# A folded two-layer network after linear attention: high parts before low parts in the second product, output copies at other places, last weight sums earlier

## The chip, the cores and the metric

The kernel runs on one core of one Trainium2 chip. The metric is the device time of one launch in microseconds (us). Before the change three runs gave 1134.80, 1135.37 and 1135.81 us, median 1135.37 us. TensorE is called PE here, its weight loads PEld, VectorE DVE, ScalarE ACT, GpSimd POOL, and the engine that issues the transfers SP.

## The reference

```python
def phi(x):
    proj = np.einsum('bhsd,df->bhsf', x, w_phi)
    proj = proj - np.max(np.abs(proj), axis=-1, keepdims=True)
    return np.concatenate([np.exp(proj), np.exp(-proj)], axis=-1)
q_p, k_p = (phi(q), phi(k))
kv = np.einsum('bhsf,bhsd->bhfd', k_p, v)
z = np.sum(k_p, axis=2)
num = np.einsum('bhsf,bhfd->bhsd', q_p, kv)
den = np.einsum('bhsf,bhf->bhs', q_p, z)[..., None] + 1e-06
x = num / den            # 4608 tokens x 512 after a transpose
h = x @ w_in             # 512 -> 2048
out = (h - np.tanh(h)) @ w_out   # 2048 -> 512
```

There are 8 batches of 8 heads with 576 positions and 64 channels; the weights of the two layers arrive in double precision and are turned into f32 on the chip.

## The kernel before, in words

A first stage does the attention and decodes the weights; its last matmul ends at about 329 us. All that the change touches lies behind it, in the two layers, which are one loop over 72 steps `s`. The 4608 tokens are 9 groups `g` of 512 (four token tiles `t` of 128), and the 2048 hidden columns are 16 tiles `f` of 128. A step is one group and one pair `j` of hidden tiles, so a group is 8 steps. Instructions stand on each engine's queue in the order in which this code writes them (the schedule is manual), and each engine takes its queue in order.

**The first product** of a step is h = x W_in. Every operand is split into a high part, rounded to the fast matmul type, and a low part, the rest; a product is high times high, high times low and low times high. Groups 0 and 1 (steps 0 to 15, "plain") do it straight: `plain`, 12 matmuls of 512 columns for each hidden tile. Groups 2 to 8 (steps 16 to 71, "folded") cut it into 2 x 2 blocks and form it from seven products instead of eight: `product`, 42 matmuls of 256 columns a step, with sums of input blocks (made on POOL, `x_sum`) and sums of weight blocks (made once on DVE, `t_add`, and split by ACT in `t_hi` and by DVE in `t_lo`). DVE puts the seven results together in PSUM (lines 884 to 893). The sums of weights for the pairs j = 0 to 7 are made in steps 9, 10, 11, 12, 13, 14, 15 and 19 by the job table at line 817.

**The activation** h - tanh(h) is worked out for two sets a step: `one` (in PSUM tile `y` or `w`) and `two` (in `x` or `v`). In a folded step set one is token tiles 0 and 1 for both hidden tiles and set two is token tiles 2 and 3; in a plain step set one is the first hidden tile for all four token tiles and set two the second. For each set ACT makes squares (`y_`, `s1_`, `s2_`), tanh (`th_`) and a mask (`mk_`), and DVE joins a polynomial with h - tanh(h) (`d1` to `d5`, lines 610 to 622). ACT then rounds the result to its high part `gh` (line 626), and POOL subtracts for the low part `gl` (line 630). The order on DVE in a step is: d3, d4, d5 of the set two of the step before; the queued weight work (`v0`: `t_lo`; `d1`: `t_add`); in a folded step the joining of the seven products; d1 to d5 of the new set one; d1, d2 of the new set two. So set two is finished in the step after.

**The second product** adds g W_out into four PSUM tiles `po`, one a token tile, over the 8 steps of a group. It is done one step late, by the function `q`: for each token tile of a set the matmuls of `gh` with the high and low weights (line 654), then those of `gl` with the high weights (line 657). 24 matmuls of 512 columns a step. In a folded step `q(one, 1)` puts tile 0 between the third-to-last and the last of the seven products:

```python
for n in (3, 2):
    product(r[n], g, j, n)
if s < NS - 1:
    q(one, 1)
product(X[:, lo_], g, j, 4)
```

and the rest follows behind the product. With the last pair of a group the four `po` are complete; `finish` copies them out at the end of that step's code, tiles 0 and 2 on DVE (line 668), 1 and 3 on ACT (line 666), and each copy is followed by its transfer to `out`. The next group's first `q` writes the same four PSUM buffers, a step later. W_out comes anew from HBM for each step of group 1 and later (`wo_fetch`, two tiles of 512 KB, four buffers).

## Time and profile before

| what | value |
|---|---|
| median of three runs | 1135.37 us (1134.80 to 1135.81) |
| time of the profiled execution | 1136.19 us |
| span of its instructions | 1134.4 us |
| PE busy | 1113.2 us, 98% |
| DVE busy | 964.5 us, 85% |
| ACT busy | 860.4 us, 76% |
| POOL busy | 525.5 us, 46% |
| granted PE clock, mean | 0.998 |

Matmuls overlap in PE's pipeline and their ends are modelled, so a busy PE is not PE at its peak, and starts are a better measure than busy time. In the views a row of the timeline is start, duration, engine, line, operation, output and inputs, with the idle time before it and what ended it in brackets; a row with x4 joins four instructions. The view of waits is who waited for whom: us in total, times, longest.

### The profile page before, as it was taken

To read this page: it belongs to the slowest core of one execution; us is meant where nothing else is said; L and a number is where in the kernel's file an instruction comes from. 1 tells how busy PE (TensorE), PEld (TensorE's weight loads), DVE (VectorE), ACT (ScalarE), POOL (GpSimd) and SP (SyncE) were. 2 spreads that over 40 slices of the span, in tenths; PEclk is the share of its full clock that TensorE was granted. 3 is DMA by queue.
4 is the path that set the end of the run, shared out by engine and by line. 5 is a ranking of instruction groups with operands and counts; after the bars stand their busy time and mean duration, and the time that the engine had idled before them with its cause. 6 is when DMAs were issued, how large, how long until landed. Compare 5 with 4: busy or idle time off the path is not lost. (4 is left out here: it accounts for less than half of the span.)

```text
span 1134.4 us, 22407 instructions
## 1 busy us (share of the span) xinstructions
PE 1113.2 (98%) x8010; PEld 894.6 (79%) x8010; DVE 964.5 (85%) x1478; ACT 860.4 (76%) x1716; POOL 525.5 (46%) x508
## 2 busy tenths in 40 slices
PE   9999999999999999999899999999999999999997
PEld 6666666666667888888788888888888888888885
DVE  6888889888879879998888888888888888888886
ACT  5888888888888877677677777777777776877765
POOL 4665665565534434443443543543543543443231
PEclk9999999999999999999999999999999999999999
DMA  5576766667624246324225325234333323422432
GB/s 162 181 242 220 237 216 211 237 219 246 204 92 153 97 155 198 112 93 151 92 82 179 106 81 185 77 111 152 108 113 127 133 96 115 161 76 95 136 105 75
DMA packets 76048, 165.41 MB, mean 146 GB/s; under 512 B 16672, under 2 KB 31392, under 8 KB 75936
## 3 DMA queue, kind: packets, MB, share of 16 engines
q1 hardware_dynamic: 75776, 163.90, 43.2%
q8 instruction: 64, 1.05, 0.4%
q14 instruction: 48, 0.39, 0.1%
q10 hardware_dynamic: 160, 0.07, 0.0%
HBM read 134.28 MB, written 29.51 MB: 144 GB/s over the span
## 5 line engine op out<-in xcount | busy, mean ns | idle before, releaser
L630 POOL TENSOR_TENSOR gl<-s,gh 128x512 fp32r<-128x512 f32 x143 | 216.9, 1517 | 325.2 <-ACT gh L626 188.5
L654 PE MATMUL po<-wo,gh 128*128 128x512 f32 x1152 | 326.8, 396 | 5.5 <-ACT mk L607 3.4
L654 PEld LDWEIGHTS po<-wo,gh 128*128 128x128 f32 x1152 | 209.3, 189 | 49.1 <-ACT mk L607 4.6
L657 PE MATMUL po<-wo,gl 128*128 128x512 f32 x576 | 197.7, 406 | 5.4 <-POOL gl L630 5.1
L626 ACT CAST gh<-s 128x512 fp32r<-128x512 f32 x144 | 89.5, 621 | 109.1 <-DVE s L622 99.1
L657 PEld LDWEIGHTS po<-wo,gl 128*128 128x128 f32 x576 | 104.8, 189 | 47.7 <-POOL gl L630 26.0
L610 DVE SCALAR_TENSOR_TENSOR s<-s,y 128x512 f32<-128x512 f32 x144 | 99.4, 690 | 47.8 <-ACT s L595 47.8
L255 DVE TENSOR_REDUCE m<-pp 128x4 f32<-128x512 f32 (+3 forms) x98 | 92.0, 940 | 40.9 <-PE pp L245 37.4
L314 POOL TENSOR_TENSOR ss<-ss,kp 128x512 f32<-128x512 f32 x96 | 122.9, 1280 | 8.0 <-ACT kp L299 3.0
L622 DVE COPY_PREDICATED s<-mk,th 128x512 f32<-128x512 uint32 x144 | 111.1, 771 | 15.2 <-ACT s L595 0.5
L595 ACT ACTIVATE s<-y,bias_t 128x512 f32<-128x512 f32 x144 | 104.3, 724 | 20.0 <-DVE s L616 11.1
L299 ACT ACTIVATE kp<-t 128x256 f32<-128x256 f32 (+2 forms) x256 | 108.8, 484 | 7.8 <-DVE t L262 7.0
L613 DVE SCALAR_TENSOR_TENSOR s<-s,s 128x512 f32<-128x512 f32 x144 | 99.7, 693 | 15.0
L607 ACT ACTIVATE mk<-y,bias_t 128x512 f32<-128x512 f32 x144 | 102.6, 712 | 0.0
L599 ACT ACTIVATE s<-y,bias_t 128x512 f32<-128x512 f32 x144 | 102.1, 709 | 0.0
L245 PEld LDWEIGHTS pp<-wph,qk 64*128 64x128 f32 x1152 | 72.1, 187 | 33.3 <-PE po L350 13.1
L262 DVE TENSOR_TENSOR t<-pp,m 128x512 f32<-128x512 f32 (+3 forms) x98 | 92.0, 941 | 3.3
L245 PE MATMUL pp<-wph,qk 64*128 64x128 f32 x1152 | 90.3, 289 | 1.2 <-PE pk L319 0.8
L591 ACT ACTIVATE y<-y 128x512 f32<-128x512 f32 x72 | 43.0, 597 | 63.9 <-DVE y L891 57.8
L713 PE MATMUL y<-xc,hl 128*128 128x256 f32 x672 | 89.3, 282 | 1.7 <-DVE th L619 1.7
L713 PEld LDWEIGHTS y<-xc,hl 128*128 128x128 f32 x672 | 84.1, 189 | 2.0 <-issue 1.6
L713 PEld LDWEIGHTS w<-xc,hl 128*128 128x128 f32 x560 | 78.0, 188 | 5.1
(396 smaller groups left out, 2242.7 us busy)
## 6 DMA issues: line engine op xcount, KB each, us to landing
wo<-wod SPq DMA_DIRECT2D x128, 512.0 KB
qk<-in_qkT SPq DMA_DIRECT2D x31, 576.0 KB
v<-in_v SPq DMA_DIRECT2D x32, 320.0 KB
rb<-rr SPq DMA_DIRECT2D x64, 144.0 KB
xs<-rb SPq DMA_DIRECT2D x32, 288.0 KB
out<-o SPq DMA_DIRECT2D x36, 256.0 KB
rawi<-in_moe_w_in SPq DMA_DIRECT2D x16, 512.0 KB
rawo<-in_moe_w_out SPq DMA_DIRECT2D x16, 512.0 KB
```

Of the source, the lines that this page charges most:

```text
L245: nc.tensor.matmul(heads[e][:, o * F : (o + 1) * F], u.qk[hs, j * P : (j + 1) * P], wph[hs, :], start=True, stop=True)
L299: nc.scalar.activation(o, x, AF.Exp, scale=1.0 - 2.0 * s)
L314: nc.gpsimd.tensor_tensor(u.ss, u.ss, u.kp[:, :, j], ALU.add)
L595: nc.scalar.activation(self.s1, self.y, AF.Square, bias=bias_t[:, 0:1])
L599: nc.scalar.activation(self.gs, self.y, AF.Square, bias=bias_t[:, 1:2])
L607: nc.scalar.activation(self.mk, self.y, AF.Relu, bias=bias_t[:, 2:3])
L613: stt(self.s1, self.gs, PC2, self.s1, ALU.add, ALU.mult)
L622: nc.vector.copy_predicated(self.gs, self.mk.bitcast(U32), self.th)
L630: (nc.vector if self.s == NS - 1 and self.tiles[0] else nc.gpsimd).tensor_tensor(self.gl, self.gs, f32(self.gh), ALU.subtract)
L654: nc.tensor.matmul(o, v.gh[:, cut], wo[g, f][:, k, :], start=not begun, stop=False)
L657: nc.tensor.matmul(o, v.gl[:, cut], wo[g, f][:, 0, :], start=False, stop=last and f == v.fs[-1])
L713: nc.tensor.matmul(o, w[:, k], x[:, a, m], start=(i == 0), stop=(i == 5))
```

## The change

Three edits, and what follows from them.

1. `q(v, part)` replaces `q(v, most)`. With part 0 it issues the matmuls of `gh` for all token tiles of a set, with part 1 those of `gl`. In a folded step part 0 of set one now stands before product 4, so two tiles stand there instead of one; part 1 of set one, then part 0 and part 1 of set two follow. This holds for the last folded step as well, which had nothing there before. In a plain step all four parts stand behind `plain`.
2. The output copies: tiles 0, 1 and 3 go to ACT and tile 2 to DVE. `finish(2)` copies tiles 0 and 1 in the step that completes them, on ACT between `gh` of the new set one and tanh of the new set two. `finish(4)` copies tiles 2 and 3 in the step after, behind `gh` of the old set two, on DVE ahead of the joining of the products. At the very end all four come after the last product.
3. The table of weight sums: the pairs 0 to 7 come in steps 9, 10, 11, 12, 13, 14, 14 and 15. Pair 6 moves from step 15 to 14 and pair 7 from step 19 to 15; its buffer is another one.

The core of the diff:

```diff
@@ -637,35 +636,38 @@
         ends = []
         mark = gp.tile([P, 1], F32, name="gate")
 
-        def q(v, most=4):
+        def q(v, part):
             if v is None:
                 return
-            g = v.g
-            for t in v.left[:most]:
-                v.left.remove(t)
-                if (g, t) not in po:
-                    po[g, t] = [ps_o.tile([P, DM], F32, tag="o", name=f"po{g}_{t}"), False]
-                o, begun = po[g, t]
-                n = v.tiles.index(t)
-                cuts = [slice((a * len(v.tiles) + n) * P, (a * len(v.tiles) + n + 1) * P) for a in range(len(v.fs))]
-                last = v.fs[-1] == NF - 1
+            g, nt = v.g, len(v.tiles)
+            last = v.fs[-1] == NF - 1
+            for n, t in enumerate(v.tiles):
+                cuts = [slice((a * nt + n) * P, (a * nt + n + 1) * P) for a in range(len(v.fs))]
+                if part == 0:
+                    begun = (g, t) in po
+                    if not begun:
+                        po[g, t] = ps_o.tile([P, DM], F32, tag="o", name=f"po{g}_{t}")
+                    for f, cut in zip(v.fs, cuts):
+                        for k in range(2):
+                            nc.tensor.matmul(po[g, t], v.gh[:, cut], wo[g, f][:, k, :], start=not begun, stop=False)
+                            begun = True
+                    continue
                 for f, cut in zip(v.fs, cuts):
-                    for k in range(2):
-                        nc.tensor.matmul(o, v.gh[:, cut], wo[g, f][:, k, :], start=not begun, stop=False)
-                        begun = True
-                for f, cut in zip(v.fs, cuts):
-                    nc.tensor.matmul(o, v.gl[:, cut], wo[g, f][:, 0, :], start=False, stop=last and f == v.fs[-1])
-                po[g, t][1] = True
+                    nc.tensor.matmul(po[g, t], v.gl[:, cut], wo[g, f][:, 0, :], start=False, stop=last and f == v.fs[-1])
                 if last:
                     ends.append((g, t))
 
-        def finish(g, t):
+        def finish(n):
+            while ends and ends[0][1] < n:
+                store(*ends.pop(0))
+
+        def store(g, t):
             pool, tag = (gp, "o") if t < 2 else (tp[0], "xs")
             o = pool.tile([P, DM], F32, tag=tag, name=f"o{g}_{t}", bufs=2)
-            if t % 2:
-                nc.scalar.copy(o, po[g, t][0])
+            if t != 2:
+                nc.scalar.copy(o, po[g, t])
             else:
-                nc.vector.tensor_copy(o, po[g, t][0])
+                nc.vector.tensor_copy(o, po[g, t])
             nc.sync.dma_start(out[(g * GT + t) * P : (g * GT + t + 1) * P, :], o)
 
         def wo_fetch(g, j):
@@ -723,7 +725,7 @@
                     i += 1
 
         def t_new(j):
-            pool, tag = (xp[0], "xc3") if j % 2 and j < NP - 1 else (tp[0], "tp")
+            pool, tag = (xp[0], "xc3") if j % 2 else (tp[0], "tp")
             t = pool.tile([P, 2, DM], F32, tag=tag, name=f"tp{j}")
             for k in range(2):
                 stage["t", 2 * j + k] = t[:, k, :]
@@ -814,7 +816,7 @@
                 job(k + 1, "v0", split_lo, *t)
         for f in range(NO):
             job(0, "d", wo_store, f, wo[0, f])
-        for j, s in enumerate((9, 10, 11, 12, 13, 14, 15, 19)):
+        for j, s in enumerate((9, 10, 11, 12, 13, 14, 14, 15)):
             job(s - 1, "d1", t_load if 2 * j < NI else t_new, j)
             job(s, "d1", t_add, j)
             job(s, "a1", t_hi, j)
@@ -875,6 +877,7 @@
             do(s, "v0")
             do(s, "d1")
             run(two, "gh_")
+            finish(4)
             run(one, "gl_")
             run(two, "gl_")
             do(s, "p0")
@@ -885,16 +888,18 @@
                 tt(K[:, 1:3, :], V.rearrange("p (a n) -> p a n", a=2), both, ALU.add)
                 for n in (3, 2):
                     product(r[n], g, j, n)
-                if s < NS - 1:
-                    q(one, 1)
+                q(one, 0)
                 product(X[:, lo_], g, j, 4)
                 tt(Y, Y, K[:, 0:2, :].rearrange("p a n -> p (a n)"), ALU.add)
                 tt(X[:, hi_], r[5], u3, ALU.add)
                 tt(r[4], r[4], u3, ALU.add)
             elif g is not None:
                 plain(X, g, 2 * j + 1)
-            q(one)
-            q(two)
+            if not fold:
+                q(one, 0)
+            q(one, 1)
+            q(two, 0)
+            q(two, 1)
             do(s, "a")
             if g is not None:
                 new, nxt = cur
@@ -905,13 +910,14 @@
                 run(new, "d3", "d4", "d5")
                 run(nxt, "y_", "s1_", "s2_")
                 run(new, "gh_")
+                finish(2)
                 do(s, "v1")
                 run(nxt, "th_", "mk_", "d1", "d2")
             do(s, "p2")
             do(s, "v")
             do(s, "a1")
-            while ends:
-                finish(*ends.pop(0))
+            if s == NS:
+                finish(4)
             if g is not None:
                 sets[s, 0], sets[s, 1] = cur
```

(The line `self.left = list(tiles)` of class Set, which `q` no longer needs, is gone too; lines behind it move up by one.)

Three places show how the instructions move. The first is PE in the middle of a folded step (step 61), between products 3 and 2 and the end of set one; po_0 and po_1 are token tiles 0 and 1, gh_0 and gl_0 the parts of set one, and x is the PSUM tile of product 4. Before:

```order
L654 MATMUL po_0_11770<-wo_12092,gh_0_12207 128x512 x2
L654 MATMUL po_0_11770<-wo_12094,gh_0_12207 128x512 x2
L657 MATMUL po_0_11770<-wo_12092,gl_0_12254 128x512
L657 MATMUL po_0_11770<-wo_12094,gl_0_12254 128x512
L713 MATMUL x_12216<-xc_4_11546,th_5642 128x256 x2
L713 MATMUL x_12216<-xc_4_11546,tl_6434 128x256
L713 MATMUL x_12216<-xc_4_11546,th_5642 128x256 x2
L713 MATMUL x_12216<-xc_4_11546,tl_6434 128x256
L654 MATMUL po_1_11786<-wo_12092,gh_0_12207 128x512 x2
L654 MATMUL po_1_11786<-wo_12094,gh_0_12207 128x512 x2
L657 MATMUL po_1_11786<-wo_12092,gl_0_12254 128x512
L657 MATMUL po_1_11786<-wo_12094,gl_0_12254 128x512
```

Now:

```order
L652 MATMUL po_0_11770<-wo_12092,gh_0_12207 128x512 x2
L652 MATMUL po_0_11770<-wo_12094,gh_0_12207 128x512 x2
L652 MATMUL po_1_11775<-wo_12092,gh_0_12207 128x512 x2
L652 MATMUL po_1_11775<-wo_12094,gh_0_12207 128x512 x2
L715 MATMUL x_12216<-xc_4_11546,th_5642 128x256 x2
L715 MATMUL x_12216<-xc_4_11546,tl_6441 128x256
L715 MATMUL x_12216<-xc_4_11546,th_5642 128x256 x2
L715 MATMUL x_12216<-xc_4_11546,tl_6441 128x256
L656 MATMUL po_0_11770<-wo_12092,gl_0_12254 128x512
L656 MATMUL po_0_11770<-wo_12094,gl_0_12254 128x512
L656 MATMUL po_1_11775<-wo_12092,gl_0_12254 128x512
L656 MATMUL po_1_11775<-wo_12094,gl_0_12254 128x512
```

The eight `gh` matmuls of both tiles stand ahead of product 4 (a row with x2 is two matmuls), and the first `gl` matmul, which was the fifth of this piece, is now the fifteenth.

The second place is the end of a group, on ACT and on DVE. ACT first (steps 16 and 17, the end of group 1): gh_0 is the high part of set one, gh_1 of set two, o_0 to o_3 the output copies, k the copy of product 1, xc the split input of group 3. Before:

```order
L626 CAST gh_0_6637<-s_0_6620 128x512
L603 ACTIVATE th_1_6639<-x_6520 128x512
L607 ACTIVATE mk_1_6641<-y_1_6631,bias_t 128x512
L666 COPY o_1_6648<-po_1_5807 128x512
L666 COPY o_3_6654<-po_3_5815 128x512
L869 COPY k_6667<-w_6665 128x256
L626 CAST gh_1_6696<-s_1_6635 128x512
L785 CAST xc_1_6753<-xr_6560 128x512
L591 ACTIVATE y_0_6755<-y_6659 128x512
```

Now:

```order
L625 CAST gh_0_6648<-s_0_6631 128x512
L668 COPY o_0_6650<-po_0_5803 128x512
L668 COPY o_1_6653<-po_1_5806 128x512
L602 ACTIVATE th_1_6656<-x_6531 128x512
L606 ACTIVATE mk_1_6658<-y_1_6642,bias_t 128x512
L871 COPY k_6672<-w_6670 128x256
L625 CAST gh_1_6701<-s_1_6646 128x512
L668 COPY o_3_6706<-po_3_5812 128x512
L787 CAST xc_1_6764<-xr_6571 128x512
L590 ACTIVATE y_0_6766<-y_6664 128x512
```

Two copies stand between gh_0 and the tanh th_1, and one between gh_1 and xc; none stands behind the mask mk_1.

DVE in the same two steps; s_1 and th_1 belong to set two, and k_... is the first joining of the products. Before:

```order
L613 SCALAR_TENSOR_TENSOR s_1_6633<-s_1_6635,s_1_6633 128x512
L668 COPY o_0_6645<-po_0_5803 128x512
L668 COPY o_2_6651<-po_2_5811 128x512
L616 SCALAR_TENSOR_TENSOR s_1_6635<-s_1_6633,x_6520 128x512
L619 TENSOR_TENSOR th_1_6639<-x_6520,th_1_6639 128x512
L622 COPY_PREDICATED s_1_6635<-mk_1_6641,th_1_6639 128x512
L884 TENSOR_TENSOR k_6667<-w_6665,k_6667 128x256
L885 TENSOR_TENSOR k_6667<-v_6666,k_6667 128x512
```

Now:

```order
L612 SCALAR_TENSOR_TENSOR s_1_6644<-s_1_6646,s_1_6644 128x512
L615 SCALAR_TENSOR_TENSOR s_1_6646<-s_1_6644,x_6531 128x512
L618 TENSOR_TENSOR th_1_6656<-x_6531,th_1_6656 128x512
L621 COPY_PREDICATED s_1_6646<-mk_1_6658,th_1_6656 128x512
L670 COPY o_2_6703<-po_2_5809 128x512
L887 TENSOR_TENSOR k_6672<-w_6670,k_6672 128x256
L888 TENSOR_TENSOR k_6672<-v_6671,k_6672 128x512
```

Two copies inside set two's chain have become one copy behind it.

The third is DVE in step 14; tp is the buffer of the weight sums, tl a low part of them. Before:

```order
L622 COPY_PREDICATED s_1_6294<-mk_1_6300,th_1_6298 128x512
L754 TENSOR_TENSOR tl_6327<-tp_6117,th_5641 128x512
L754 TENSOR_TENSOR tl_6329<-tp_6117,hl_4827 128x512
L741 TENSOR_TENSOR tp_6226<-wi_1413,wi_1124 128x256
L741 TENSOR_TENSOR tp_6226<-wi_1413 128x256
L741 TENSOR_TENSOR tp_6226<-wi_1413,tp_6226 128x256
L741 TENSOR_TENSOR tp_6226<-wi_1124,tp_6226 128x256
L610 SCALAR_TENSOR_TENSOR s_0_6382<-s_0_6382,y_0_6380 128x512
```

Now:

```order
L621 COPY_PREDICATED s_1_6295<-mk_1_6301,th_1_6299 128x512
L756 TENSOR_TENSOR tl_6328<-tp_6117,th_5641 128x512
L756 TENSOR_TENSOR tl_6330<-tp_6117,hl_4827 128x512
L743 TENSOR_TENSOR tp_6226<-wi_1413,wi_1124 128x256
L743 TENSOR_TENSOR tp_6226<-wi_1413 128x256
L743 TENSOR_TENSOR tp_6226<-wi_1413,tp_6226 128x256
L743 TENSOR_TENSOR tp_6226<-wi_1124,tp_6226 128x256
L743 TENSOR_TENSOR tp_6227<-wi_1990,wi_1701 128x256
L743 TENSOR_TENSOR tp_6227<-wi_1990 128x256
L743 TENSOR_TENSOR tp_6227<-wi_1990,tp_6227 128x256
L743 TENSOR_TENSOR tp_6227<-wi_1701,tp_6227 128x256
L609 SCALAR_TENSOR_TENSOR s_0_6387<-s_0_6387,y_0_6385 128x512
```

Four more subtractions stand ahead of set one's chain. In step 15, in the same way, four tl rows stand ahead of four tp rows, where two and four stood.

More of the change, by code (lines that the diff above doesn't have):

```diff
@@ L583, in __init__ @@
                 self.nm = f"{s}_{half}"
-                self.left = list(tiles)
             def tile(self, tag, dt=F32, bufs=1):
```

## The prediction

> **What bounds the kernel now.** I read the page first, then the waits of the folded steps, then the timeline of two steps in their middle.
>
> ```profile
> PE 1113.2 (98%) x8010; PEld 894.6 (79%) x8010; DVE 964.5 (85%) x1478; ACT 860.4 (76%) x1716; POOL 525.5 (46%) x508
> ```
>
> PE looks like the bound. The waits of the stretch from 500 to 1108 us say something else:
>
> ```profile
> ACT y L591 <- DVE y L891: 56.5, 55, 3.3
> DVE s L610 <- ACT s L595: 37.6, 55, 0.7
> PEld po L657 <- POOL gl L630: 23.3, 48, 1.0
> ```
>
> DVE's only regular wait there is for ACT (L595), and what ACT had waited for is DVE (L891). PE waits for POOL's gl at L657, once a step. The timeline shows which of the two loops is closed:
>
> ```profile
> 991.79 1.67 POOL L630 TENSOR_TENSOR gl<-s,gh 128x512 fp32r<-128x512 f32 x1 [1.56 <-ACT gh L626]
> 992.46 1.08 PE L654 MATMUL po<-wo,gh 128*128 128x512 f32 x4
> ...
> 993.52 0.74 PE L657 MATMUL po<-wo,gl 128*128 128x512 f32 x2
> ...
> 994.09 0.39 PE L713 MATMUL x<-xc,th 128*128 128x256 f32 x2
> ...
> 994.79 1.09 PE L654 MATMUL po<-wo,gh 128*128 128x512 f32 x4
> ...
> 995.72 0.63 PE L657 MATMUL po<-wo,gl 128*128 128x512 f32 x2
> 995.76 0.70 DVE L891 TENSOR_TENSOR y<-y,k 128x512 f32<-128x512 f32 x1
> ...
> 996.19 1.10 PE L654 MATMUL po<-wo,gh 128*128 128x512 f32 x4
> ...
> 996.55 0.60 ACT L591 ACTIVATE y<-y 128x512 f32<-128x512 f32 x1 [0.81 <-DVE y L891]
> 996.82 0.43 DVE L893 TENSOR_TENSOR x<-x,k 128x256 f32<-128x256 f32 x1
> ...
> 997.94 0.69 DVE L610 SCALAR_TENSOR_TENSOR s<-s,y 128x512 f32<-128x512 f32 x1 [0.69 <-ACT s L595]
> 998.99 1.10 PE L713 MATMUL w<-xc,hl 128*128 128x256 f32 x8
> ...
> 1002.33 0.59 ACT L603 ACTIVATE th<-x 128x512 f32<-128x512 f32 x1
> ...
> 1003.78 0.68 DVE L619 TENSOR_TENSOR th<-x,th 128x512 f32<-128x512 f32 x1
> ...
> 1008.72 0.69 DVE L610 SCALAR_TENSOR_TENSOR s<-s,y 128x512 f32<-128x512 f32 x1 [0.68 <-ACT s L595]
> ...
> 1009.75 1.10 PE L713 MATMUL w<-xc,hl 128*128 128x256 f32 x8
> ```
>
> L891 lets ACT go, ACT's y and s1 let L610 go, and from L610 DVE works through to its next L891 with no idle time listed. That ring takes 1008.72 - 997.94 = 10.78 us and has no PE in it. PE's step takes 1009.75 - 998.99 = 10.76 us. Tile 1 shows the usual pace: four matmuls at L654 from 994.79 to 995.72, 0.93 us (0.233 each), two at L657 to 996.19, 0.47; product 4 before it has six in 0.70 (994.09 to 994.79). At tile 0 the four take 1.06 (0.13 waited for gl, which ends at 993.46) and the two 0.57 (0.10 to start again). So PE could do a step in about 10.53 us and is held back to DVE's 10.78. **DVE with ACT sets the folded steps; PE's wait for gl is what it looks like from PE.** The time of the change is therefore read from what it does to DVE's ring, and then from the end of the program.
>
> **The change part by part.** *High parts before low parts.* Count and shape of the matmuls stay. The first gl matmul of set one moves behind eight instead of four gh matmuls and product 4, so gl may come 0.93 + 0.70 = 1.6 us later. PE gains 0.23 us a step for two or three steps, until it waits for gh, or for the bank of product 4: free at the end of L619, 1004.46, and wanted at 992.46 + 10.76 + 8 x 0.233 = 1005.08. That 0.6 us of room is used up, and the bank is late next. Then it goes at DVE's rate again. Product 4 comes later in PE's step by 0.23 us (8 x 0.233 instead of 994.09 - 992.46), and L893, which needs it, starts only at 996.82, over a microsecond behind its end. I cost this edit at 0 in the folded steps; if DVE's cover were gone, it would be the first rival below.
>
> In the plain steps PE does set the pace up to about step 8, and one stall there goes directly:
>
> ```profile
> 343.78 0.50 PE L657 MATMUL po<-wo,gl 128*128 128x512 f32 x1 [0.49 <-POOL gl L630]
> ```
>
> The listed 0.49 us counts from the modelled end of the matmul before; with the usual overlap of 0.16 (0.63 for two that start 0.47 before the next) and 0.10 to start again it is 0.75. gl has 1.4 us more there, so -0.75 us from step 1 to step 8.
>
> *Copies, plain end of group (step 8).* There the last four matmuls complete all four tiles, and the view shows ACT waiting for them even at the end of its queue:
>
> ```profile
> 422.44 0.58 ACT L666 COPY o<-po 128x512 f32<-128x512 f32 x1
> 423.81 0.59 ACT L666 COPY o<-po 128x512 f32<-128x512 f32 x1 [0.79 <-PE po L657]
> ```
>
> Tile 3 could be copied at 423.81, tile 1 by two matmuls (0.47) earlier, less the 0.75 gained: 422.6. Only then come tanh and mask, which DVE's L619 needs; that eats most of the 0.75, and DVE's copy of tile 2 comes 0.6 us on top behind it. I take +0.2 us for steps 1 to 9 together, bounds -0.8 and +1.2.
>
> *Copies, folded end of group (seven, steps 16 to 64).*
>
> ```profile
> 951.62 0.70 DVE L891 TENSOR_TENSOR y<-y,k 128x512 f32<-128x512 f32 x1
> ...
> 958.86 1.28 DVE L668 COPY o<-po 128x512 f32<-128x512 f32 x2
> 959.30 1.06 ACT L666 COPY o<-po 128x512 f32<-128x512 f32 x2
> ...
> 963.41 0.70 DVE L891 TENSOR_TENSOR y<-y,k 128x512 f32<-128x512 f32 x1
> ```
>
> DVE's ring is 963.41 - 951.62 = 11.79 us here, 1.01 over the usual: two copies of 0.60 to 0.64, less 0.2 because they fill the wait between two dependent operations. One copy is left, where nothing can be filled: +0.60. Two copies on ACT, about 1.0 us, now stand ahead of tanh (L603). From its end, 1002.92, to L619 at 1003.78 is 0.86 us of room, so L619 is late by 0.1 to 0.2. The tiles that ACT copies are long complete in a folded step (PE finishes set one over 2 us before the step ends). Sum 0.75 instead of 1.01: -0.27 x 7 = **-1.9 us**, bounds -4.2 (no lateness and the copy filled in) and +1.8 (all of the two copies late: 0.60 + 0.66 - 1.01 = 0.25 each). ACT's copy of tile 3 fits into the 0.81 us that it waits for L891. SP's output transfers now come in pairs, and the weight fetch of the step after stands behind two instead of four; in the waits of 500 to 1108 us PE has none for a transfer.
>
> *Weight sums.* What goes away is seen at DVE's L610 of set two in steps 19, 20 and 21:
>
> ```profile
> 538.39 0.69 DVE L610 SCALAR_TENSOR_TENSOR s<-s,y 128x512 f32<-128x512 f32 x1
> ...
> 551.62 0.70 DVE L610 SCALAR_TENSOR_TENSOR s<-s,y 128x512 f32<-128x512 f32 x1
> ...
> 563.63 0.67 DVE L610 SCALAR_TENSOR_TENSOR s<-s,y 128x512 f32<-128x512 f32 x1
> ```
>
> 13.23 and 12.01 us where 10.78 is usual: **-3.7 us**. What is added lies in steps 14 and 15, in which DVE is already full (it has no idle time listed from step 9 on, so whatever is added runs to the end):
>
> ```profile
> 485.39 0.68 DVE L754 TENSOR_TENSOR tl<-tp,th 128x512 fp32r<-128x512 f32 x1
> 486.35 1.48 POOL L630 TENSOR_TENSOR gl<-s,gh 128x512 fp32r<-128x512 f32 x1 [1.94 <-issue]
> 486.60 1.51 DVE L741 TENSOR_TENSOR tp<-wi,wi 128x256 f32<-128x256 f32 x1
> ...
> 488.37 0.88 DVE L741 TENSOR_TENSOR tp<-wi,tp 128x256 f32<-128x256 f32 x2
> 489.16 0.68 DVE L610 SCALAR_TENSOR_TENSOR s<-s,y 128x512 f32<-128x512 f32 x1
> ```
>
> Two L754 take 486.60 - 485.39 = 1.21 us. The first L741 takes 1.51 where 0.41 is usual, because POOL's gl runs meanwhile; the last two take 0.79. So four more L741 in step 14 behind the blocked one: 2 x 0.79 = 1.5. In step 15 two more L754, and the blocked instruction is now an L754; a block costs the rest of gl, whatever it hits:
>
> ```profile
> 352.17 1.80 DVE L687 TENSOR_TENSOR wo<-wo,wo 128x512 fp32r<-128x512 f32 x1
> ```
>
> (this one, of 512 columns, took 1.80 for 0.69 beside another gl: 1.1 as well). So +1.2, and 0.1 for ACT's two more casts. **+2.8 us**, bounds +2.0 and +5.0 (two more blocks of 1.1).
>
> *The end.* PE waits for the last gh and then has 24 matmuls:
>
> ```profile
> 1122.34 1.19 PE L654 MATMUL po<-wo,gh 128*128 128x512 f32 x4 [2.14 <-ACT gh L626]
> ...
> 1125.07 1.91 PE L654 MATMUL po<-wo,gh 128*128 128x512 f32 x4
> ...
> 1127.63 1.11 PE L654 MATMUL po<-wo,gh 128*128 128x512 f32 x4
> ...
> 1129.99 0.63 PE L657 MATMUL po<-wo,gl 128*128 128x512 f32 x2
> ```
>
> 8.3 us from 1122.34 to 1130.62, though 24 x 0.233 and 0.4 for the last one's passage are 6.0: a wait for gl, and a stretch near 1125 in which four matmuls took 1.91 instead of 1.1 after PE's idling. Now both high parts come while gl is made, so the wait goes; but PE reaches this point earlier (its eight gh matmuls of the set before now fill the wait for the last bank, and nothing follows) and idles some 4 us. I take a slow stretch of the same kind and a little longer: 7.7 us, -0.6, and +0.3 because tiles 2 and 3 now leave together. **-0.3 us**, bounds -2.3 (no slow stretch) and +2.4 (all 24 at the slow 0.43).
>
> Sum: 0.2 - 1.9 - 3.7 + 2.8 - 0.3 = **-2.9 us**. The profiled execution took 1136.19 us (span 1134.4), 0.8 above the median of the runs; its 1133.3 is 1132.5 beside the median of 1135.37.
>
> **The rivals.** *PE sets the folded steps after all.* Then 0.23 us goes in each of the 55 folded steps but the first, -12.4 us, to 1123.0. For it: the 98% and a wait in every step. Against it: the ring without PE. It needs that ring to shorten by itself. 5%.
>
> *The gains are eaten.* Only the difference of large terms is left over: if the copies on ACT delay L619 fully (+3.7 on my term) or two more blocks fall into steps 14 and 15 (+2.2), the time is 1134.7 to 1136.2. 24%.
>
> *The end goes slow.* PE's longer idling before the last 24 matmuls lets all of them run at 0.43: +2.7 on my term, 1135.2. For it: the row at 1125.07 follows an idling of only 2.14 us. Against it: 1127.63 is fast again 5.3 us after PE's restart, and now PE is denser. 11%. The Trainium skill, "TensorE: Matmul & The Clock Gate", Part 1 (the HAM clock gate), speaks for this side: an idle window of about 3.4 us halves PE's clock until a busy window has passed. By it, one or two windows run slow, an estimate of 1.7 to 3.4 us of loss where I count 1.7; the row at 1125.07 agrees with a halving.
>
> *Slower: ACT waits inside the ring.* The copies of tiles 0 and 1 stand ahead of tanh. If they wait for PE at folded ends too, as the row at 423.81 does at a plain one, each us of that wait is a us of the ring, seven times. With 0.8 us, 5.6 - 2.9 = +2.7, 1138; it decides from about 0.75. Against it: PE is through with these two tiles while set two's twelve matmuls (2.8 us) are still to come in the step, and ACT reaches the copies some 3 us into the next step (th at 1002.33, step at 998.99). 8%.
>
> **How the numbers follow.** My forecast, a small gain by DVE's sum, has 52%; its own range is 1130.6 to 1134.4. The predicted time is **1132.5 us**. For 8 in 10 the range takes in the eaten gains and the slow end, and leaves the two far rivals out: 1129.8 to 1136.3. About 0.2% (2.3 us, below 1133.1 or above 1137.6) is what a measurement can tell from no change. Faster by more: the forecast's lower two thirds and more, 0.40, the PE rival 0.05, and a share of the eaten gains where other terms help, 0.08: 0.53. Slower by more: the ACT rival's 0.08 and a little of the slow end, 0.09 together. Between: 0.38.
>
> **What would show it.** Right: PE's waits for gl at L657 (L656 then) nearly gone, yet its step in a folded group still 10.75 to 10.8 us, with waits for gh or for L619 in their place; L610 still waiting 0.69 for L595; the ring at a group's end about 11.5 instead of 11.79; steps 19 and 20 like the others; steps 14 and 15 about 1.3 us longer each; a longer idle time of PE before the last gh. Wrong: folded steps of 10.55 us (then PE was the bound), a wait of ACT's copies for PE in folded steps, or steps 14 and 15 with several long L741 or L754 rows.

## The result: 5.5 us slower, and the profile after

The changed kernel takes **1140.65 us** (median of five runs, 1140.1 to 1141.49), the kernel before 1135.13 us beside it: a ratio of 1.0052, 95% interval 1.0037 to 1.0066. The prediction was 1132.5 us, its range 1129.8 to 1136.3. It was wrong, in sign and in range.

The first lines of the page and the waits from 500 to 1113 us, after the change (L652 and L656 are the matmuls of high and low parts, L609, L612, L615, L618 and L621 VectorE's five steps d1 to d5 of the activation, L602 tanh, L668 ScalarE's output copies, L893 the sum that lets ScalarE go, L715 the folded products):

```profile
span 1139.8 us, 22413 instructions
PE 1116.5 (98%) x8010; PEld 897.3 (79%) x8010; DVE 961.4 (84%) x1469; ACT 864.6 (76%) x1725; POOL 524.3 (46%) x508
...
ACT y L590 <- DVE y L893: 54.1, 55, 2.5
DVE s L609 <- ACT s L594: 37.6, 55, 0.7
PEld x L715 <- DVE th L618: 24.9, 55, 1.7
...
DVE s L615 <- ACT th L602: 6.3, 7, 0.9
```

TensorE's 48 waits for GpSimd's low part are gone from this list. In their place it waits 55 times, 24.9 us, for the bank of product 4 (L618 frees it). VectorE's 55 waits of 0.7 us for ScalarE's s1 stand as before: the ring still sets the pace. New is one row: VectorE's **d3** waits for tanh, seven times, up to 0.9 us, once at each folded group end.

A table by step shows where the time went. The time of a step runs from VectorE's d1 of set two in the step before it to d1 of set two in the step itself; all are from the profiled executions. Five of the kernels are the experiments below: e1 is the changed kernel with the old copies, e2 the copies alone, e3 the changed kernel with ScalarE's copies of tiles 0 and 1 behind the mask, e5 the order of high and low parts alone, e8 is e3 with tile 2 on ScalarE too.

| Steps | before | after | e1 | e2 | e3 | e5 | e8 |
|---|---|---|---|---|---|---|---|
| 6 + 7 | 21.65 | 20.83 | 20.82 | 21.03 | 20.83 | 20.83 | 20.84 |
| 9 (plain group end) | 11.64 | 13.30 | 12.08 | 11.96 | 11.05 | 12.07 | 11.03 |
| 14 + 15 (weight sums arrive) | 22.10 | 24.79 | 24.63 | 22.10 | 24.76 | 22.10 | 24.78 |
| 17 (group end) | 11.78 | 12.53 | 11.80 | 12.19 | 11.75 | 11.79 | 10.88 |
| 19 + 20 (weight sums leave) | 25.24 | 21.54 | 21.56 | 25.21 | 21.57 | 25.19 | 21.56 |
| 23 | 10.80 | 12.12 | 10.81 | 12.08 | 12.12 | 10.79 | 11.13 |
| 49 (group end, as 25, 41, 57, 65) | 11.78 | 12.18 | 11.79 | 12.18 | 11.42 | 11.79 | 10.86 |
| 67 | 10.81 | 12.13 | 10.83 | 12.15 | 12.13 | 10.82 | 10.80 |

After against before: the low part's wait -0.82, step 9 +1.66, step 12 -0.52 (0.35 of it is a stalled instruction, explained below, that only the kernel before has there), the weight sums +2.69 and -3.70, seven group ends +0.40 each, which is +2.80 (0.35 of step 17 is something else, below). Stalled VectorE instructions in single steps, 23 and 67 above all, make +3.35 after and 1.43 before, +1.92. These sum to +4.03; +0.23 at the start and small rests make 4.49 up to d1 of set two in step 70 (1110.68 before, 1115.17 after), and what follows it is 0.91 longer: 5.4 us of span.

One **folded group end** after the change, VectorE's and ScalarE's rows in order of time:

```profile
956.03 0.69 DVE L609 SCALAR_TENSOR_TENSOR s<-s,y 128x512 f32<-128x512 f32 x1 [0.68 <-ACT s L594]
...
960.43 1.06 ACT L668 COPY o<-po 128x512 f32<-128x512 f32 x2
960.49 0.69 DVE L612 SCALAR_TENSOR_TENSOR s<-s,s 128x512 f32<-128x512 f32 x1
961.38 0.61 ACT L602 ACTIVATE th<-x 128x512 f32<-128x512 f32 x1
962.08 0.69 DVE L615 SCALAR_TENSOR_TENSOR s<-s,x 128x512 f32<-128x512 f32 x1 [0.91 <-ACT th L602]
962.69 0.68 DVE L618 TENSOR_TENSOR th<-x,th 128x512 f32<-128x512 f32 x1
...
964.13 0.67 DVE L670 COPY o<-po 128x512 f32<-128x512 f32 x1
...
968.22 0.69 DVE L609 SCALAR_TENSOR_TENSOR s<-s,y 128x512 f32<-128x512 f32 x1 [0.68 <-ACT s L594]
```

The two copies are not held up by TensorE. They take 1.06 us ahead of tanh, tanh ends at 961.99, and the next row of VectorE starts at 962.08. That row is d3 (L615), which does not read tanh; d4 (L618), which does, follows without a wait. The reason stands in the instruction lists, where the waits of each instruction are written beside it. VectorE's set two of a usual step, before the change:

```
L610 SCALAR_TENSOR_TENSOR s_1_10821<-s_1_10821,y_1_10819 128x512 [waits Activation_49]
L613 SCALAR_TENSOR_TENSOR s_1_10821<-s_1_10823,s_1_10821 128x512 [waits DVE_49,Activation_49]
L616 SCALAR_TENSOR_TENSOR s_1_10823<-s_1_10821,x_10707 128x512 [waits DVE_49,Activation_49]
L619 TENSOR_TENSOR th_1_10827<-x_10707,th_1_10827 128x512
L622 COPY_PREDICATED s_1_10823<-mk_1_10829,th_1_10827 128x512 [waits DVE_49,Activation_49]
```

L619 carries no wait at all: what it needs of ScalarE has been waited for at L616, one instruction earlier. It stands so in both kernels.

The **plain group end** after the change, same two engines:

```profile
420.27 0.62 ACT L625 CAST gh<-s 128x512 fp32r<-128x512 f32 x1
420.85 0.69 DVE L612 SCALAR_TENSOR_TENSOR s<-s,s 128x512 f32<-128x512 f32 x1
422.57 1.08 ACT L668 COPY o<-po 128x512 f32<-128x512 f32 x2 [1.68 <-PE po L656]
423.53 0.62 ACT L602 ACTIVATE th<-x 128x512 f32<-128x512 f32 x1
424.24 0.69 DVE L615 SCALAR_TENSOR_TENSOR s<-s,x 128x512 f32<-128x512 f32 x1 [2.69 <-ACT th L602]
```

Here the copies do wait for TensorE, 1.68 us, and VectorE stands for 2.69 us.

**Step 23**, and a usual step ahead of it (22), the start of GpSimd's gl and of VectorE's d2 of set two:

```profile
575.50 0.69 DVE L612 SCALAR_TENSOR_TENSOR s<-s,s 128x512 f32<-128x512 f32 x1
575.67 1.68 POOL L629 TENSOR_TENSOR gl<-s,gh 128x512 fp32r<-128x512 f32 x1 [1.62 <-ACT gh L625]
...
586.47 1.30 POOL L629 TENSOR_TENSOR gl<-s,gh 128x512 fp32r<-128x512 f32 x1 [1.56 <-ACT gh L625]
586.65 1.67 DVE L612 SCALAR_TENSOR_TENSOR s<-s,s 128x512 f32<-128x512 f32 x1 [0.46 <-ACT gh L625]
```

Usually d2 starts 0.17 us ahead of gl, takes 0.69, and gl takes 1.68. In step 23 d2 starts late by 0.36; gl is first, takes 1.30, and d2 takes 1.67. The 0.97 us that d2 loses are lost to the ring. The Trainium skill, "SBUF — State Buffer", section "SBUF: two separate sides", says that VectorE with two SBUF inputs and GpSimd share a port pair which the one that starts first keeps for the whole instruction; these four rows agree.

**The end**, TensorE's rows after the change:

```profile
1126.82 3.78 PE L652 MATMUL po<-wo,gh 128*128 128x512 f32 x8 [4.00 <-ACT gh L625]
1130.40 1.91 PE L656 MATMUL po<-wo,gl 128*128 128x512 f32 x4
1132.10 2.32 PE L652 MATMUL po<-wo,gh 128*128 128x512 f32 x8
1134.27 1.10 PE L656 MATMUL po<-wo,gl 128*128 128x512 f32 x4
```

From the last group's first matmul to the end of its last these are 8.55 us, where before had 8.28. The granted clock is the third number from the right in the next rows, three stretches of the kernel before and one of the changed kernel:

```profile
1122.40:1124.20 1.80, 1.19 (x5) 0.67 (x5) 1.67 (x3) 0.99 (x2) 1.67 (x1) 1.00 0.02 5
1124.30:1127.60 3.30, 3.30 (x8) 2.56 (x9) 2.09 (x4) 0.62 (x1) 0.00 (x0) 0.50 0.02 5
1127.70:1130.60 2.90, 2.90 (x13) 2.03 (x11) 0.69 (x1) 0.58 (x1) 0.00 (x0) 1.00 0.48 181
```

```profile
1126.00:1132.70 6.70, 5.88 (x14) 4.63 (x15) 4.05 (x7) 3.33 (x7) 1.67 (x1) 0.50 0.01 2
```

The clock is full or half. Its mean is 0.83 from 1120 to 1130 us before and 0.76 from 1122 to 1136 after, so it was half for 10 x 0.17 / 0.5 = 3.4 us before and for 14 x 0.24 / 0.5 = 6.7 us after.

### The profile page after: what moved, and what is told of

Its sections match the earlier page's. It is cut to its first block, busy times and chain, and to the rows that moved or that the text cites. A ratio compares the mean times of both kernels' runs of the same rounds, so it can differ in the third digit from the quotient of the medians.

```text
span 1139.8 us, 22413 instructions
## 1 busy us (share of the span) xinstructions
PE 1116.5 (98%) x8010; PEld 897.3 (79%) x8010; DVE 961.4 (84%) x1469; ACT 864.6 (76%) x1725; POOL 524.3 (46%) x508
## 4 chain that ended last, share of the span: by engine, by line
DVE 47%; PE 37%; ACT 10%; issue 5%; DVEq 1%; ACTq 0%; POOL 0%; POOLq 0%
DVE s L621 8%; PE pp L245 7%; DVE s L615 7%; DVE s L612 7%; PE pc L305 6%; DVE th L618 6%; DVE s L609 6%; PE po L350 6%; ACT s L594 4%; DVE y L893 3%; DVE k L888 3%; PE po L652 3%; PE pd L365 3%; ACT y L590 3%; PE ptt L272 2%
## 5 line engine op out<-in xcount | busy, mean ns | idle before, releaser
L652 PE MATMUL po<-wo,gh 128*128 128x512 f32 x1152 | 297.0, 400 | 6.8 <-ACT gh L625 5.0
L652 PEld LDWEIGHTS po<-wo,gh 128*128 128x128 f32 x1152 | 213.0, 189 | 57.4 <-ACT gh L625 7.1
L656 PE MATMUL po<-wo,gl 128*128 128x512 f32 x576 | 158.4, 397 | 0.0
L609 DVE SCALAR_TENSOR_TENSOR s<-s,y 128x512 f32<-128x512 f32 x144 | 98.8, 686 | 46.6 <-ACT s L594 46.6
L621 DVE COPY_PREDICATED s<-mk,th 128x512 f32<-128x512 uint32 x144 | 111.1, 772 | 14.9
L656 PEld LDWEIGHTS po<-wo,gl 128*128 128x128 f32 x576 | 104.8, 189 | 21.3
L612 DVE SCALAR_TENSOR_TENSOR s<-s,s 128x512 f32<-128x512 f32 x144 | 101.7, 706 | 16.0 <-ACT gh L625 1.4
L715 PE MATMUL y<-xc,hl 128*128 128x256 f32 x672 | 89.8, 283 | 4.5 <-DVE th L618 4.5
L715 PEld LDWEIGHTS y<-xc,hl 128*128 128x128 f32 x672 | 84.0, 189 | 6.1 <-PE v L715 4.8
L715 PEld LDWEIGHTS w<-xc,hl 128*128 128x128 f32 x560 | 77.9, 188 | 5.1
```

The source lines that it names most:

```text
L609: stt(self.s1, self.s1, PC1, self.y, ALU.add, ALU.mult)
L612: stt(self.s1, self.gs, PC2, self.s1, ALU.add, ALU.mult)
L621: nc.vector.copy_predicated(self.gs, self.mk.bitcast(U32), self.th)
L652: nc.tensor.matmul(po[g, t], v.gh[:, cut], wo[g, f][:, k, :], start=not begun, stop=False)
L656: nc.tensor.matmul(po[g, t], v.gl[:, cut], wo[g, f][:, 0, :], start=False, stop=last and f == v.fs[-1])
L715: nc.tensor.matmul(o, w[:, k], x[:, a, m], start=(i == 0), stop=(i == 5))
```

## The experiments

Two theories to begin with. **Theory 1**: the copies cost it, because two of them stand ahead of tanh on ScalarE and VectorE waits for tanh at d3. **Theory 2**: the order of high and low parts costs it.

**e1, the old copies in the changed kernel.**

```
-            if t != 2:
+            if t % 2:
...
-            finish(4)
...
-                finish(2)
...
-            if s == NS:
-                finish(4)
+            finish(4)
```

> The changed kernel with the output copies put back as they were before (at the end of a step, tiles 0 and 2 on VectorE, 1 and 3 on ScalarE); high parts first and the new weight sums stay. Theory 1 (the copies cost it: two ScalarE copies stand ahead of tanh, and VectorE's third polynomial step of set two, not the subtraction behind it, waits for tanh): VectorE's step 9 goes from 13.30 back to about 11.6 us, the folded group ends from 12.18 to 11.8, step 17 from 12.53 to 11.8; 1.7 + 0.75 + 6 x 0.40 = 4.8 us less than the changed kernel, about 1135.8 if the two long steps 23 and 67 (12.12 where 10.8 is usual) stay, about 1133.3 if they go too. Theory 2 (it is the order of high and low parts, by the end of the program and by VectorE and GpSimd meeting at other places): 1139 or more, steps 9 and 17 as in the changed kernel or moved elsewhere.

Measured: 1136.81 us, ratio 1.0014 (1.0005 to 1.0023), 3.8 us below the changed kernel. Steps 17, 23, 49 and 67 are back at their old values, step 9 is 12.08. It did not get to 1133.3: a new step of the kind of step 23, step 50, takes 12.13 us, steps 22, 33, 39 and 66 hold stalls of about 0.35 us each, and steps 9 and 12 stay about 0.5 us above what the sum had for them. Theory 1 holds for the larger part.

**e2, the copies alone**, the same edit the other way round in the kernel before.

> The kernel before with the copies alone moved as in the change. Theory 1: slower by 4 to 6 us, 1139 to 1141: step 9 about 13.3 or a little more (ScalarE's copies wait for TensorE), seven folded group ends at 12.2. Theory 2: within 1.5 us of before, group ends at 11.5 to 11.8.

Measured: 1140.36 us, ratio 1.0046 (1.0032 to 1.0060). The copies alone cost almost the whole of what the change costs. Group ends are 12.18, as expected, which is 2.8 us; a further 2.6 us are steps 23 and 67, where moving the copies shifts VectorE's list so that a stall meets d2 (e6 below undoes this by another shift). Step 9 is 11.96 and not 13.3: with each tile's low parts right behind its high parts, ScalarE waits only 0.28 us for TensorE:

```profile
421.13 1.29 ACT L670 COPY o<-po 128x512 f32<-128x512 f32 x2 [0.28 <-PE po L657]
```

So the 1.66 us of step 9 come from two edits together: high parts first completes all four tiles only in the last four matmuls, and early copies then wait for them ahead of tanh. Alone they cost 0.32 (e2) and 0.43 (e5).

**e3, ScalarE's copies of tiles 0 and 1 behind the mask.**

```
                 run(new, "gh_")
-                finish(2)
                 do(s, "v1")
                 run(nxt, "th_", "mk_", "d1", "d2")
+                finish(2)
```

> The changed kernel with ScalarE's copies of tiles 0 and 1 behind tanh and mask of the second set instead of ahead of them. Theory 1: they leave VectorE's ring; ScalarE idles 1.41 us there before the next high part, which covers 1.06 us; a folded group end goes from 12.18 to 10.78 + 0.60 for the one VectorE copy = 11.4 us, step 9 to under 12. 1140.65 - 7 x 0.8 - 1.5 = about 1133.5, less if the two long steps 23 and 67 go away too (1131). Theory 2 (the copies cost as much at any place, since ScalarE has no room): 1139 or more, with the ring's wait moved to the high part.

Measured: 1133.23 us, ratio 0.9980 (0.9972 to 0.9989): 7.4 us less than the changed kernel, 1.9 less than before, by moving one line. Steps 23 and 67 stay long. A group end of it:

```profile
950.50 0.69 DVE L609 SCALAR_TENSOR_TENSOR s<-s,y 128x512 f32<-128x512 f32 x1 [0.69 <-ACT s L594]
...
955.78 0.69 DVE L615 SCALAR_TENSOR_TENSOR s<-s,x 128x512 f32<-128x512 f32 x1
956.00 1.06 ACT L668 COPY o<-po 128x512 f32<-128x512 f32 x2
...
961.91 0.69 DVE L609 SCALAR_TENSOR_TENSOR s<-s,y 128x512 f32<-128x512 f32 x1 [0.69 <-ACT s L594]
```

961.91 - 950.50 = 11.41 us: the usual 10.78 and VectorE's one copy. The same copies, 1.06 us, cost nothing here.

**e10, the copies between tanh and mask**, to see which of the two is wanted early.

```
-                finish(2)
-                do(s, "v1")
-                run(nxt, "th_", "mk_", "d1", "d2")
+                run(nxt, "th_")
+                finish(2)
+                do(s, "v1")
+                run(nxt, "mk_", "d1", "d2")
```

> The changed kernel with ScalarE's copies of tiles 0 and 1 between tanh and mask. If the late tanh alone made the group ends long (VectorE's third polynomial step waits for it, and the mask, wanted two instructions later, has about 1 us of room more), a folded group end is 11.4 to 11.5 us as in e3, and the time within 0.7 us of e3's (ratio 0.998 to 0.9986). If the mask is wanted as early as tanh, 12.1 as in the changed kernel.

Measured: 1134.33 us, ratio 0.9995 (0.9986 to 1.0005), above the 0.998 to 0.9986 expected. The group ends are 11.42, so tanh alone made them long. What it loses to e3 lies in the last group (8.51 us instead of 7.41: the half clock lasts 6.7 us here and 3.4 in e3) and in step 9 (11.98 instead of 11.05), where the copies still wait for TensorE and the mask behind them:

```profile
422.57 1.08 ACT L668 COPY o<-po 128x512 f32<-128x512 f32 x2 [1.18 <-PE po L656]
423.53 0.74 ACT L606 ACTIVATE mk<-y,bias_t 128x512 f32<-128x512 f32 x1
424.30 0.75 DVE L621 COPY_PREDICATED s<-mk,th 128x512 f32<-128x512 uint32 x1 [1.33 <-ACT mk L606]
```

**e4, the weight sums alone**: `(9, 10, 11, 12, 13, 14, 15, 19)` becomes `(9, 10, 11, 12, 13, 14, 14, 15)` in the kernel before, with its tile tag.

> The kernel before with the two tables of the weight sums alone changed. Both theories: steps 19 and 20 shorter by 2.46 and 1.24 us, steps 14 and 15 longer by 1.49 and 1.19: -1.0 us, about 1134.1. If it comes out 1 us or more above that, VectorE and GpSimd meet at a new place, as in steps 23 and 67 of the changed kernel.

Measured: 1135.18 us, ratio 0.9996 (0.9988 to 1.0005), 1.1 us above what was expected. It is not a new meeting of VectorE and GpSimd: d1 of set two in step 70 starts 1.12 us earlier than before (1109.56 against 1110.68), as it should. The end gives it back: the last group takes 9.52 us where before had 8.28, with the same instructions. Four of the eleven runs take 1133.6 to 1133.9 us and the profiled one is the slowest, 1136.44, so the profile speaks for the slow end of the spread only. The half clock lasts 6.8 us (13 x 0.26 / 0.5) where before had 3.4:

```profile
1121.21 1.20 PE L654 MATMUL po<-wo,gh 128*128 128x512 f32 x4 [2.13 <-ACT gh L626]
...
1126.59 1.91 PE L654 MATMUL po<-wo,gh 128*128 128x512 f32 x4
...
1130.11 0.62 PE L657 MATMUL po<-wo,gl 128*128 128x512 f32 x2
```

```profile
1118.00:1131.00 13.00, 10.00 (x29) 7.04 (x27) 7.50 (x12) 5.46 (x10) 1.67 (x1) 0.74 0.12 44
```

**e5, the order alone**: e1 with the old table of weight sums.

> The kernel before with the high parts first alone. Theory 1 (the copies cost it, the order is free in the folded steps): steps 6 and 7 of VectorE 0.4 us shorter each, folded steps still 10.78, the last 24 matmuls 0.3 us longer: 1135 +- 0.8, plus up to 1.3 us where a stalled VectorE instruction lets GpSimd start first. Theory 2 (the order costs): 1137 or more with folded steps above 10.78.

Measured: 1137.51 us, ratio 1.0015 (1.0006 to 1.0024). The order does not touch the usual folded step (10.78). It gains 0.82 in steps 6 and 7, loses 0.43 in step 9, and loses 1.33 in step 50, where a stalled d2 starts behind gl. The edit leaves VectorE's instructions as they are, 1478, but its list has six more records of waits (651 instead of 645), so the stalled places fall on other instructions. Theory 2 needed folded steps above 10.78 and falls: what the order costs here is mostly that one meeting, which the next run shows to be movable.

**e6, two fillers.** By now it had been seen that one VectorE instruction in some steps starts 0.35 us late with nothing to wait for. The changed kernel with two instructions more on VectorE, long before these steps:

```
+        pad = gp.tile([P, 1], F32, name="pad")
+        for _ in range(2):
+            nc.vector.memset(pad, 0.0)
```

> The changed kernel with two one-column memsets on VectorE early in the program, and nothing else. VectorE stalls 0.35 us at about every 167th of its instructions; in the changed kernel numbers 722 and 1388 are the second polynomial step of set two, which then starts behind GpSimd's gl instead of ahead of it and takes 1.66 instead of 0.69 us. Theory A (position in VectorE's own list): with the list moved by two, the stall falls on the predicated copy of set one, ahead of gl; steps 23 and 67 go from 12.12 to about 11.15 us, 1.9 us less than the changed kernel, about 1138.7. Theory B (the stall belongs to a time or to a step, not to a place in the list): steps 23 and 67 stay at 12.12, 1140.7.

Measured: 1138.93 us, ratio 1.0026 (1.0016 to 1.0035), against 1.0052 of the changed kernel. Steps 23 and 67 go from 12.12 and 12.13 to 10.77 and 10.82; I had left 0.35 us of stall in each, and even that is not seen there: the places of the list that stalled now hold d1 of set two, which does not stall (the last section says which instructions do). In step 67, d2 is ahead of gl again and takes its usual time:

```profile
1070.40 0.69 DVE L612 SCALAR_TENSOR_TENSOR s<-s,s 128x512 f32<-128x512 f32 x1
1070.56 1.68 POOL L629 TENSOR_TENSOR gl<-s,gh 128x512 fp32r<-128x512 f32 x1 [5.93 <-ACT gh L625]
```

d1 of set two in step 70 comes 2.27 us earlier than in the changed kernel, for two memsets of one column. The long steps belong to a place in VectorE's list, not to the work of these steps (theory A). The rest of what the time shows is the clock again: the last group takes 7.37 instead of 8.55 us, with a half clock of 3.4 instead of 6.7 us.

**e7, filling TensorE's last wait** in e3.

```
+            if s == NS:
+                warm = ps_x.tile([P, GN], F32, tag="w", name="warm")
+                for _ in range(15):
+                    nc.tensor.matmul(warm, th[0][:, 0:P], wo[NG - 1, NF - 1][:, 0, :], start=True, stop=True)
```

> The kernel of e3 (copies behind the mask) with 15 matmuls more into a PSUM tile that nobody reads, in TensorE's wait of 4.0 us ahead of the last group's high part. Theory A (TensorE's clock halves by the idling): the eight matmuls behind the wait take about 2.0 us instead of 3.59, the last ones wait for the last gh only; about 1 us from the last gh on is saved, 0.8 to 1.6 us less than e3's 1133.2. Theory B (the slow stretch is the wait for gl or a cost of restarting): no change.

Measured: 1131.9 us, ratio 0.9961 (0.9949 to 0.9974) against 0.9980 (0.9972 to 0.9989) of e3; the intervals just overlap. The end of it:

```profile
1114.82 3.66 PE L901 MATMUL warm<-wo,th 128*128 128x512 f32 x15
1118.99 2.12 PE L652 MATMUL po<-wo,gh 128*128 128x512 f32 x8 [0.51 <-ACT gh L625]
1120.95 1.10 PE L656 MATMUL po<-wo,gl 128*128 128x512 f32 x4
1122.63 2.13 PE L652 MATMUL po<-wo,gh 128*128 128x512 f32 x8 [0.57 <-ACT gh L625]
1124.59 1.10 PE L656 MATMUL po<-wo,gl 128*128 128x512 f32 x4
```

In e3 the first of these groups was:

```profile
1119.78 3.59 PE L652 MATMUL po<-wo,gh 128*128 128x512 f32 x8 [4.01 <-ACT gh L625]
```

The eight matmuls take 2.12 instead of 3.59 us, and the last group 6.70 (1118.99 to 1125.69) instead of 7.41; the granted clock is 1.00 all through. The profile shows theory A; the time itself supports it only weakly.

**e8, tile 2 on ScalarE too** (`if t != 2 or g < NG - 1:` in e3).

> The kernel of e3 with tile 2 copied by ScalarE as well (the last group apart), right behind tile 3. VectorE's list has no copy left in a group's end; ScalarE idles 0.93 us there, of which 0.6 was VectorE's copy. If VectorE's ring alone decides: 10.78 + 0.2 = 11.0 us instead of 11.4 at seven group ends, 0.4 x 7 = 2.8 us less than e3, 1130.4; the stalled places move too (one instruction fewer per group), up to 1.9 us either way. If ScalarE is the tighter one there: no gain.

Measured: 1127.97 us, ratio 0.9923 (0.9911 to 0.9936). The group ends fall to 10.81 to 10.88, 0.1 above a usual step and better than the 11.0 expected; and with one VectorE instruction less in each group the stalls miss d2 of set two: steps 23 and 67 take 11.13 and 10.80. ScalarE has just enough room. At the group end from 946.75, its wait ahead of y is gone, and s1 comes only 0.05 us later than usual:

```profile
954.75 1.07 ACT L668 COPY o<-po 128x512 f32<-128x512 f32 x2
955.39 0.70 DVE L893 TENSOR_TENSOR y<-y,k 128x512 f32<-128x512 f32 x1
955.70 0.63 ACT L787 CAST xc<-xr 128x512 fp32r<-128x512 f32 x1
956.22 0.61 ACT L590 ACTIVATE y<-y 128x512 f32<-128x512 f32 x1
...
957.62 0.69 DVE L609 SCALAR_TENSOR_TENSOR s<-s,y 128x512 f32<-128x512 f32 x1 [0.73 <-ACT s L594]
```

**e9, e8 and e7 together.**

> e8 with the 15 matmuls of e7 in TensorE's last wait. The two act at different places (group ends, end of the program), so their gains should add: 0.9923 and 0.9961 - 0.9980 = -0.0019 give 0.9904 of the kernel before, 1124.5 to 1126.5 by the clock of that chip. If the filler only moved the slow stretch, no better than e8.

Measured: 1125.92 us, ratio 0.9921 (0.9909 to 0.9934), the fastest kernel of the study, 0.8% below the kernel before. The expected 0.9904 was missed, and by the ratio it is no faster than e8; that the gains add is not shown by the times. In the profiles the last group takes 6.71 us where e8 has 8.37, and the span is 2.0 us shorter.

**e11 and e12, the old order in e9** (`pair` issues the high and then the low parts of each tile it is given).

```
-                q(one, 0)
+                if s < NS - 1:
+                    pair(one, (0,))
                 product(X[:, lo_], g, j, 4)
...
-            q(one, 1)
-            q(two, 0)
-            q(two, 1)
+            pair(one, range(1 if fold and s < NS - 1 else 0, 4))
+            pair(two, range(4))
```

> e9 with the high and low parts of each token tile together, as before the change; VectorE's and GpSimd's lists stay as in e9. If VectorE's ring decides the folded steps, these stay as in e9, and only the waits for the low part come back: steps 6 and 7 of VectorE 0.8 us longer together, of which step 9 gives 0.4 back, and the last 24 matmuls wait once for a low part (up to 0.6): 0.2 to 1.0 us slower than e9. If the order itself cost something in the folded steps, it is faster than e9.

e11 leaves out six matmuls of step 16 (the second product of tiles 2 and 3 for one set), so e12 was run in its place; e11 took 1126.55 us, ratio 0.9928.

> e11 with nothing left out: e9 with high and low parts of each token tile together, as before the change. As e11: steps 6 and 7 of VectorE 0.8 us longer together, folded steps as in e9, one wait for a low part in the last 24 matmuls: 0.2 to 1.5 us slower than e9.

Measured for e12: 1127.27 us, ratio 0.9930 (0.9916 to 0.9943). In its profile steps 6 and 7 take 0.75 us longer than in e9, step 18 0.31, and the usual folded steps 10.78 in both. That is the direction expected; the intervals overlap, so the profile shows the worth of the order and the times do not. The filler was made for e9's wait: with the old order TensorE comes later to it, and the first matmul of the last group follows the filler without any wait.

## Why the prediction was wrong

**What bounds the kernel: right.** VectorE's ring sets the folded steps. TensorE's wait for gl went away and it waits for the bank of product 4 instead, as foretold; a usual folded step stayed at 10.78, and s1 is waited for 55 times as before. The rival in which TensorE sets the folded steps falls with that.

**High parts first: right, but for its place in the list.** 0 in the folded steps, and -0.82 for the predicted -0.75 in the plain ones. That the same edit can cost 1.33 us in one step by shifting VectorE's list (e5) was in no rival.

**Weight sums: right.** -3.70 for -3.7, +2.69 for +2.8. (The three rows of what goes away are set two's d1 of steps 18, 19 and 20, and not of 19 to 21; the differences are right.)

**Copies at a folded group end: the step that failed.** The prediction took the room of tanh "from its end, 1002.92, to L619 at 1003.78", 0.86 us, because L619 reads tanh. The wait stands at L616. In the kernel before, that one starts here:

```profile
1003.18 0.69 DVE L616 SCALAR_TENSOR_TENSOR s<-s,x 128x512 f32<-128x512 f32 x1
```

So the room was 1003.18 - 1002.92 = 0.26 us, and the two copies, 1.06 us together, make VectorE 0.80 late instead of 0.1 to 0.2. With this one number the prediction's own sum becomes 0.60 + 0.80 - 1.01 = +0.39 per group end; measured is +0.40. The rest of that term was right: one copy on VectorE costs 0.63 (e3), and the copies do not wait for TensorE there. Seven times the difference, from -1.9 to +2.8, is 4.7 us. The bound of +1.8 was too low by a slip of its own: "all of the two copies late" is 1.06 us and not 0.66, so it should have been 0.60 + 1.06 - 1.01 = 0.65 each or +4.6, and the measured +2.8 lies below that.

**Copies at the plain group end: mis-sized.** The prediction put the copies at 422.6 and they started at 422.57, but it let this eat "most of the 0.75", with +0.2 for steps 1 to 9. Measured: -0.82 + 1.66 = +0.84, inside the bounds of -0.8 and +1.2. The wait again counts from d3: L615 at 424.24 where the row before it, L612, starts at 420.85.

**The end: mis-sized.** -0.3 predicted, +0.9 measured. I took one slow stretch and 7.7 us for the last group's matmuls; there were two windows of half clock and 8.55 us. In six other kernels with the same instructions there it took 7.37 to 8.51 us, 7.4 with one window and 8.1 to 8.5 with two. So the rival of the slow end came true in part: its mechanism, and about 0.9 of the 2.7 us it was priced at. Against the kernel before, these matmuls make 0.27 of the +0.9; 0.64 comes behind the last matmul, 4.43 us to the end of the span instead of 3.79, where the prediction had 0.3. The order makes that: e5, with the old copies, has 4.38.

**Not in the sum: stalled instructions**, +1.92 us. The kernel before shows them too, at harmless places (steps 22, 33, 44 and 55, about 0.35 us each); I had not asked what they would hit when the list moves. The four terms that were off make 4.7 + 0.6 + 1.2 + 1.9 = 8.4 us, the way from the -2.9 predicted to the +5.5 measured; step 12 and the small rests nearly cancel.

**The rivals.** The nearest was the one on the slower side, ScalarE waiting inside the ring, held at 8%. Its price was about right (5.6 us for 0.8 us of lateness at seven ends), its cause was not: it needed copies that wait for TensorE at folded ends, and what decided was the length of the copies against a room that had been read from the wrong instruction. The eaten gains named the right term too, with a bound that was too low.

## What to carry to other kernels

Read the room ahead of a wait from the instruction that carries the wait, not from the one that reads the data: the list of waits tells it, and one instruction of 0.6 us decided the sign here. Work that is off the critical path belongs behind everything the critical engine still wants from the engine that does it; the same two copies cost 0.8 us a group ahead of tanh and nothing behind the mask. Where two engines start within 0.2 us of each other on something they cannot share, a small delay anywhere upstream may turn their order round, so compare several placements before crediting a change with the last microsecond.

## What the runs showed of the hardware

**VectorE stalls about 0.35 us at fixed places of its list.** A wait that an instruction needs can stand in the trace as a record of its own ahead of it. Counting all of VectorE's records, these waits among them, the late instructions are number 703, 831, 959, 1087, 1215, 1343, 1471, 1599, 1727, 1855 or 1983: 128 apart, counted from 0, in all fourteen kernels (0.35 to 0.37 us late; three further rows, number 1670 of e2 and 855 of e11 and e12, 0.28 us late, do not fit). Without the records of waits the count gave the "about every 167th" that stands ahead of e6. These eleven numbers are 154 places in the fourteen traces, and the kind of record there decides. At 61 of them stands an instruction with a record of a wait right ahead of it, and all 61 start about 0.4 us behind that record where 0.04 is usual. At the other 93 stands a record of a wait, or an instruction without one right ahead of it, and none shows the stall. What causes it no run here tells.

**Which of two engines starts first decides 1 us.** d2 (two SBUF inputs) takes 0.69 us ahead of gl and 1.67 behind it, gl 1.68 and 1.30.

**The clock after idling comes back in steps of 3.4 us.** Ahead of the last matmul the clock was half for 3.4 us in before, e2, e3 and e6, for 6.7 to 6.8 in the changed kernel, e1, e4, e5, e8 and e10, and never in e7 and e9, which fill the wait; nothing lay between. The kernel before and e4 have the same instructions there and differ by one such step, 1.24 us of time. The Trainium skill, "TensorE: Matmul & The Clock Gate", Part 1, has the clock follow windows of about 3.4 us that run on freely and do not start anew with a kernel; the lengths in the twelve profiles agree with that. The idle window of about 3.4 us that the prediction names was not needed here: the wait ahead of the half clock was 2.14 us in the kernel before and 2.13 in e4. In e5 the clock is half once more, in the stretch from 551.2 to 554.5 us, behind a wait of 2.13 us, and its steps 19 and 20 take 25.19 us where before, at full clock, took 25.24: VectorE's ring does not feel it.

The kernel before shows the effect with nothing changed at all. It ran again beside each of four groups of experiments, and its fourteen runs with a mean clock of 1.000 took on average 0.6 to 1.8 us less than those with 0.998 of the same group. This makes any comparison of two kernels with such a wait uncertain by about 1 us.
